# Attention's second product of batch 0 in plain float32 for all six head pairs

## The chip, the cores and the metric

The kernel runs on one core of one Trainium2 chip. The metric is the device time of one execution in microseconds (us), the median over the runs that were made of it. A profile is one execution taken by the hardware profiler; its own time stands beside its span, from the first to the last instruction. The names of the engines are those of the profile: PE is TensorE's matmul side, PEld its weight loads, DVE is VectorE, ACT is ScalarE, POOL is GpSimd, and SP is the queue that issues every DMA of this kernel.

## The reference

Attention over 4 batches, 12 heads, 448 positions and 64 channels, with RMS-normalised queries and keys; its output, 1792 rows of 768, then goes through two blocks of matrix products. Cut to what matters here:

```python
scores = scale * np.matmul(q_n, k_n.transpose(0, 1, 3, 2))
scores = scores - np.max(scores, axis=-1, keepdims=True)
attn = np.exp(scores)
attn = attn / (np.sum(attn, axis=-1, keepdims=True) + 1e-09)
attn_out = np.matmul(attn, v)            # "the second product"
x = attn_out.transpose(0, 2, 1, 3).reshape(B * S, H * D)
x = ((x @ w1) * (x @ w2)) @ w3 @ w_out   # layers 1 and 2
h = x @ w_in
out = (h * np.clip(h + 3.0, 0.0, 6.0) / 6.0) @ w_out2
```

## The kernel before, in words

The 48 heads are taken as 24 pairs (`NP`), six pairs (`HP`) to a batch, so pairs 0 to 5 are batch 0. The attention loop goes by steps: pair i has its eight score tiles (two heads, four chunks of 112 queries) in steps 8i to 8i+7, its seven transposes (`trans`) from step 8i+8 and its seven second products (`pv`) from step 8i+10. In each step the code writes down: the two score matmuls (L561, L562), DVE's scaling and row maximum (L568, L575), ACT's exponential (L580) of the step before, four 112 by 112 transposes on PE (L587) into a PSUM bank of the tag "t" (two banks), their way out of PSUM, and one second product.

Precision is kept by splitting. A float32 operand is written as a high part in float32r, rounded by ACT, and a low part in float32r, the rest, and matmuls are taken on the parts. For the second product of a pair that is not in `FULL` this means: ACT copies the transposed attention into `xh` (L596, function `thi`), DVE subtracts that from PSUM into `xl` (L606, `tlo`), `vsplit` makes V's high part on ACT (L549) and its low part on POOL (L550) from the tile `vr` into the tile `vo`, and `pv` multiplies 128 columns of V (high and low side by side) with `xh` (L639) and with `xl` (L640). Of seven products of a pair the fourth (`kb == 3`) holds the last 64 keys of both heads, 64 rows each (L627). Afterwards ACT copies one half of the result (L647, `xcopy`) and DVE adds the other half to it (L655, `xadd`).

For a pair in `FULL` the same functions take a shorter way: V is loaded straight into `vo` in float32 (`load_v`), `vsplit`, `tlo` and `xadd` do nothing, `xh` is float32, and `pv` is one float32 matmul with 64 columns of V (L635; for the fourth product L621). The tile tag `vo` has two buffers, `vr` has one.

Between the steps the code writes "filler": the products of the two linear layers that follow. First come the products of w3 and w_out (`wprime`, 128 by 384 columns, L81 to L83 on `woh`), then layers 1 and 2 of a batch (`layer1`, `layer2`, 448 columns, L81 to L83 on `xhl`), at a rate of so many us of matmul for each step. Layer 1 of batch 0 begins only when `wprime` is through and pairs 0 to 5 are ready (`xout` L664, `xsplit` L308). The weights for the filler arrive as 8-byte numbers and are converted on ACT (L137, L138), DVE (L140, L143), ACT (L203 or L287) and POOL (L205 or L289).

The order of the instructions on each engine is not the written one alone: a scheduler sets it by simulated times, buffers and the links that `issue_after` adds. After about 640 us the attention is over and the third and fourth layers take the rest.

Of the kernel before, what the change touches and what calls it, by code (L numbers as in the profile page):

```python
# [24 lines left out]
HP = H // 2  # L25
# [11 lines left out]
NH = DM // 2  # L37
XB = 7
TAGS = ("s", "t", "v", "f")
FULL = (0, 1)  # L40
LG = 8
AHEAD = 3
K3 = 12
# [4 lines left out]
def fused_kernel(ctx: ExitStack, tc: tile.TileContext, nat, qT, kT, vin, gq, gk,  # L48
# [358 lines left out]
    def attention(ap, rate):  # L407
        def full(i):
            return i in FULL

# [556 lines left out]
```

## Time and profile before

| what | value |
|---|---|
| median of 3 runs | 1238.3 us (1236.92 to 1243.6) |
| profiled execution: its own time | 1239.83 us |
| profiled execution: its span | 1238.1 us, mean granted clock 0.98 |
| PE busy | 1168.1 us, 94% of the span |
| DVE busy | 751.1 us, 61% |
| ACT busy | 727.8 us, 59% |
| POOL busy | 463.9 us, 37% |

Busy times are averages over stages with different limits. Matmuls are pipelined: one that is recorded as 0.37 us long can be followed by the next after 0.21 us, so the distance from start to start says what one costs, and not its recorded length.

### The profile page before, as it was taken

The numbers are of one execution on the slowest core, as the hardware profiler recorded it, in microseconds if no ns is written. First come the engines' busy times: TensorE is split into PE (matmuls) and PEld (weight loads), VectorE is DVE, ScalarE is ACT, GpSimd is POOL, SyncE is SP. The second block draws the span as 40 slices with busy tenths as digits, with TensorE's granted clock in tenths as the row PEclk, the third lists the DMA queues.
The fourth block names the chain that finished last, engine by engine and source line by source line (L and its number), as shares of the span: only waits on it lengthen the run. The fifth ranks groups of instructions, "written<-read, shape, count | busy, mean of one in ns | idle before, by whom it ended". The sixth has DMA issues, their size and how long they took to land.

```text
span 1238.1 us, 16937 instructions
## 1 busy us (share of the span) xinstructions
PE 1168.1 (94%) x5868; PEld 1024.0 (83%) x5868; DVE 751.1 (61%) x1474; ACT 727.8 (59%) x1401; POOL 463.9 (37%) x316
## 2 busy tenths in 40 slices
PE   3698998988899999999999999989999999999998
PEld 2457877777789999889998998779999999999997
DVE  6977988998767787667624436774433333343332
ACT  6887788888857677666534435664533443343332
POOL 3534234553522213221020005445545445455442
PEclk9798998998999999999999999999999999999999
DMA  7667666797987777764469963440200020001001
GB/s 277 204 215 237 193 184 205 247 291 260 307 299 239 224 238 224 244 224 174 145 253 410 342 236 127 154 153 1 89 1 1 1 90 1 1 1 45 1 1 45
DMA packets 64694, 203.73 MB, mean 165 GB/s; under 512 B 8544, under 2 KB 25440, under 8 KB 64608
## 3 DMA queue, kind: packets, MB, share of 16 engines
q1 hardware_dynamic: 64608, 202.65, 48.4%
q8 instruction: 46, 0.75, 0.2%
q14 instruction: 40, 0.33, 0.1%
HBM read 173.93 MB, written 28.68 MB: 164 GB/s over the span
## 4 chain that ended last, share of the span: by engine, by line
PE 62%; DMA 4%; DVE 4%; ACT 3%; issue 2%; POOL 0%; SPq 0%; ACTq 0%; POOLq 0%; DVEq 0%
PE bank L81 7%; PE bank L83 7%; PE bank L82 7%; PE acc L81 6%; PE acc L82 6%; PE acc L83 6%; PE h L81 5%; PE h L82 5%; PE h L83 5%; PE bank L587 2%; PE bank L561 1%; PE bank L562 1%; DVE wf L143 1%; PE bank L639 1%; PE bank L640 1%
## 5 line engine op out<-in xcount | busy, mean ns | idle before, releaser
L835 POOL TENSOR_TENSOR wis<-wf,wis 128x768 fp32r<-128x768 f32 x63 | 120.9, 1919 | 234.3 <-ACT wis L834 234.3
L907 DVE SCALAR_TENSOR_TENSOR u<-u,h 128x448 f32<-128x448 f32 x64 | 39.6, 619 | 212.3 <-ACT u L906 212.3
L835 POOL TENSOR_TENSOR wos<-wf,wos 128x768 fp32r<-128x768 f32 x64 | 119.0, 1860 | 98.1 <-ACT wos L834 98.1
L580 ACT ACTIVATE PP<-PP,mx 112x448 f32<-112x448 f32 x192 | 127.4, 665 | 38.9 <-DVE mx L575 34.3
L568 DVE CUSTOM_DVE_ANT_0 PP<-bank,rb,rq 112x448 f32<-112x448 f32 x192 | 129.3, 677 | 32.0 <-PE bank L562 25.2
L81 PE MATMUL bank<-xhl,ws 128*128 128x448 f32 x384 | 143.1, 373 | 3.7 <-ACT ws L287 2.2
L83 PE MATMUL bank<-xhl,ws 128*128 128x448 f32 x384 | 141.5, 369 | 3.7 <-POOL ws L289 3.7
L82 PE MATMUL acc<-g,wos 128*128 128x448 f32 x384 | 142.6, 371 | 2.3 <-DVE g L911 2.3
L83 PE MATMUL acc<-g,wos 128*128 128x448 f32 x384 | 141.9, 369 | 0.0
L82 PE MATMUL bank<-xhl,ws 128*128 128x448 f32 x384 | 141.2, 368 | 0.0
L81 PE MATMUL acc<-g,wos 128*128 128x448 f32 x384 | 138.8, 374 | 2.5 <-ACT g L910 2.5
L81 PE MATMUL h<-x2h,wis 128*128 128x448 f32 x378 | 139.2, 368 | 0.6 <-DVE u L907 0.6
L83 PE MATMUL h<-x2h,wis 128*128 128x448 f32 x378 | 137.7, 364 | 2.2 <-POOL wis L835 2.2
L82 PE MATMUL h<-x2h,wis 128*128 128x448 f32 x378 | 139.0, 368 | 0.0
L906 ACT ACTIVATE u<-h,half 128x448 f32<-128x448 f32 x64 | 40.6, 634 | 141.1 <-PE h L83 141.1
L911 DVE TENSOR_TENSOR g<-u,g 128x448 fp32r<-128x448 f32 x64 | 99.5, 1554 | 35.4 <-ACT g L910 35.4
L606 DVE TENSOR_TENSOR xl<-bank,xh 128x448 fp32r<-128x448 f32 x142 | 87.4, 617 | 30.0 <-ACT xh L596 28.3
L834 ACT ACTIVATE wos<-wf 128x768 fp32r<-128x768 f32 x64 | 54.0, 844 | 84.2 <-PE acc L83 84.0
L587 PEld LDWEIGHTS bank<-ident,PP 112*128 112x128 f32 x672 | 79.3, 143 | 28.0 <-issue 9.7
L596 ACT ACTIVATE xh<-bank 128x448 fp32r<-128x448 f32 (+1 forms) x156 | 83.1, 539 | 32.4 <-PE bank L587 30.8
L587 PE MATMUL bank<-ident,PP 112*128 112x112 f32 x672 | 96.0, 266 | 6.5 <-DVE xl L606 5.2
L561 PE MATMUL bank<-K,Q 128*112 128x448 f32 x192 | 77.1, 403 | 24.1 <-DVE mx L568 12.7
(128 smaller groups left out, 2755.7 us busy)
## 6 DMA issues: line engine op xcount, KB each, us to landing
ws<-w12d SPq DMA_DIRECT2D x48, 768.0 KB
ws<-wpd SPq DMA_DIRECT2D x32, 768.0 KB
raw<-in_w_dram SPq DMA_DIRECT2D x32, 384.0 KB
w12d<-ws SPq DMA_DIRECT2D x16, 768.0 KB
wr<-in_win_dram SPq DMA_DIRECT2D x16, 768.0 KB
wr<-in_wo_dram SPq DMA_DIRECT2D x16, 768.0 KB
qr<-in_qT_dram SPq DMA_DIRECT2D x24, 448.0 KB
kr<-in_kT_dram SPq DMA_DIRECT2D x24, 448.0 KB
```

Of the source, the lines that this page charges most:

```text
L81: nc.tensor.matmul(ps, lh, rh, start=first, stop=False)
L82: nc.tensor.matmul(ps, lh, rl, start=False, stop=False)
L83: return nc.tensor.matmul(ps, ll, rh, start=False, stop=last)
L561: nc.tensor.matmul(ps[:CP, :S], qs, k1[:, j, :], start=True, stop=False)
L568: anchors[8 * i + s].append(nc.vector.tensor_tensor_reduce(out=T["PP", i][:, c, sl], in0=ps[:CP, :S], in1=T["rb", i][:, sl], op0=ALU.mult, ...
L580: anchors[8 * i + s].append(nc.scalar.activation(v, v, AF.Exp, bias=T["m", i][:, 8 + s : 9 + s], accum_out=T["sum", i][:, s : s + 1]))
L587: nc.tensor.transpose(ps[:, c * CP : c * CP + CP], src[:, c, kb * P : kb * P + P], ident[:CP, :CP])
L596: nc.scalar.activation(hi, ps, AF.Copy)
L606: nc.vector.tensor_sub(lo, ps, hi)
L834: nc.scalar.activation(t[:, 0, :], wf[q], AF.Copy)
L835: nc.gpsimd.tensor_sub(t[:, 1, :], wf[q], t[:, 0, :])
L911: nc.vector.tensor_sub(g[:, 1, :], u, g[:, 0, :])
```

## The change

`FULL` names the pairs that take the float32 way. It held pairs 0 and 1; now it holds all six pairs of batch 0. Pairs 6 to 23 stay as they were, and no other line is touched.

```diff
-FULL = (0, 1)
+FULL = range(HP)
```

## Rows read from the trace of the kernel before

**Rows 1.** Stretches: length, then PE, PEld, DVE, ACT, POOL busy, clock, DMA.

```profile
110.00:140.00 30.00, 30.00 (x178) 27.76 (x177) 19.86 (x48) 19.37 (x42) 11.34 (x10) 1.00 0.77 233
140.00:182.00 42.00, 39.94 (x228) 34.10 (x227) 38.18 (x99) 33.45 (x74) 13.60 (x11) 1.00 0.58 180
182.00:200.00 18.00, 15.56 (x68) 11.85 (x67) 16.66 (x39) 13.42 (x33) 8.43 (x7) 0.72 0.53 174
200.00:350.00 150.00, 134.25 (x690) 110.11 (x689) 129.56 (x319) 127.08 (x286) 74.50 (x63) 0.98 0.82 273
350.00:640.00 290.00, 288.61 (x1599) 261.13 (x1598) 201.45 (x524) 188.26 (x406) 65.50 (x56) 1.00 0.66 218
```

**Rows 2.** Timeline of PE, a float32 product of pair 0: start, length, what.

```profile
74.31 0.33 PE L82 MATMUL bank<-woh,w 128*128 128x384 f32 x1
74.49 0.34 PE L83 MATMUL bank<-woh,w 128*128 128x384 f32 x1
74.76 0.97 PE L635 MATMUL bank<-xh,vo 128*64 128x448 f32 x2
75.65 0.60 PE L587 MATMUL bank<-ident,PP 112*128 112x112 f32 x4
```

**Rows 3.** Timeline of PE, split products of pair 3.

```profile
136.71 0.45 PE L640 MATMUL bank<-xl,vo 128*128 128x448 f32 x1
137.00 0.37 PE L639 MATMUL bank<-xh,vo 128*128 128x448 f32 x1
137.21 0.36 PE L561 MATMUL bank<-K,Q 128*112 128x448 f32 x1
```

**Rows 4.** Timeline of PE, the fourth product: pair 1 in float32, pair 4 split.

```profile
85.93 0.97 PE L621 MATMUL bank<-xh,vo 64*64 64x448 f32 x4
86.83 0.60 PE L587 MATMUL bank<-ident,PP 112*128 112x112 f32 x4
...
163.12 0.47 PE L627 MATMUL bank<-xh,vo 64*128 64x448 f32 x2
163.51 0.60 PE L587 MATMUL bank<-ident,PP 112*128 112x112 f32 x4
```

**Rows 5.** Groups by line, 100 to 200 us: busy, mean ns | idle before.

```profile
L606 DVE TENSOR_TENSOR xl<-bank,xh 128x448 fp32r<-128x448 f32 x29 | 17.9, 616 | 2.4 <-ACT xh L596 2.1
...
L550 POOL TENSOR_TENSOR vo<-vr,vo 128x512 fp32r<-128x512 f32 x4 | 5.5, 1379 | 31.4 <-DMA rsb<-rsd 14.1 <-ACT vo L549 10.1 <-issue 7.3
```

**Rows 6.** Waits of PE, 100 to 200 us: total, times, longest.

```profile
PE bank L587 <- DVE xl L606: 2.6, 3, 1.7
PE bank L640 <- DVE xl L606: 1.4, 2, 0.7
PE bank L83 <- POOL w L205: 1.1, 1, 1.1
PE bank L561 <- DVE mx L568: 0.8, 2, 0.4
```

**Rows 7.** Stretches at the low clock, and what lies before them.

```profile
102.00:107.60 5.60, 5.52 (x19) 5.33 (x20) 5.57 (x14) 5.60 (x11) 1.45 (x1) 0.50 0.54 177
186.40:196.40 10.00, 9.21 (x31) 6.77 (x32) 8.73 (x20) 7.29 (x19) 5.21 (x5) 0.50 0.68 236
97.20:102.10 4.90, 1.86 (x8) 0.68 (x6) 4.90 (x14) 4.85 (x13) 1.84 (x2) 0.88 0.79 270
183.60:186.40 2.80, 1.25 (x6) 0.65 (x4) 2.80 (x5) 2.80 (x7) 1.93 (x2) 0.97 0.65 169
```

**Rows 8.** Timeline of DVE and POOL: one DVE operation twice, and POOL beside it.

```profile
100.16 1.24 DVE L487 TENSOR_SCALAR rq<-rr 112x16 f32<-112x16 f32 x1
...
148.79 0.16 DVE L487 TENSOR_SCALAR rq<-rr 112x16 f32<-112x16 f32 x1
...
99.79 1.59 POOL L550 TENSOR_TENSOR vo<-vr,vo 128x512 fp32r<-128x512 f32 x1 [2.34 <-ACT vo L549]
```

**Rows 9.** Waits of the SP queue, 100 to 200 us.

```profile
SPq L89 <- DVE Q L534: 7.7, 1, 7.7
```

## Prediction

> **What bounds the kernel now.** I read the stretches first, because the mean over the span hides the stages [rows 1]. The products that change, of pairs 2 to 5, stand between 102 and 195 us. There PE is busy for 30.00 of 30 us from 110 to 140 and for 39.94 of 42 us up to 182, so PE sets the pace. From 182 to 200 us PE has only 15.56 of 18 us, at a mean clock of 0.72. DVE is nearly as full: 38.18 of 42 and 16.66 of 18 us. From 200 to 350 us no engine is full (PE 134.25, DVE 129.56, ACT 127.08 of 150), and from 350 to 640 us PE has 288.61 of 290. Next I read what PE waits for in this stage [rows 6]: 5.9 us in all, 4.0 of them for DVE's `xl`, which is what the change takes away. Then the clock [rows 7]: two stretches, 5.6 and 10.0 us long, run at 0.50, that is the lower level of 1.2 GHz. Before the first PE worked 1.86 of 4.90 us, before the second 1.25 of 2.80. So the stage is bound by PE, with gaps that DVE causes and that are followed by a slow clock. The change gives PE more work and DVE less, and the question is which counts for more.
>
> I take a delay or a gain at 200 us to reach the end in full: layer 1 of batch 0 can't begin before the filler of this stage is through, and from 350 us on PE has no room to catch up [rows 1].
>
> **PE's new work.** In `FULL` a product is one float32 matmul, recorded as two. From its start to the next instruction it takes 75.65 - 74.76 = 0.89 us, and it begins 0.27 us after a filler matmul, where filler follows filler after 0.18 us: 0.09 us at its entry [rows 2]. A split product is two matmuls, one after transposes with 0.29 us to the next and one with 0.21 us: 0.50 us, or 0.42 us where both follow other matmuls [rows 3]. So a product costs 0.89 - 0.50 = 0.39 us more at the least, 0.89 + 0.09 - 0.42 = 0.56 us at the most. I take 0.50, nearer the upper end, because both kinds of entry (after transposes and after filler) occur in this stage and the shown float32 product has filler ahead of it. The fourth product of a pair has four short matmuls in 0.90 us, where the split way has two passes of 0.39 us: 0.12 us more [rows 4]. A pair has six of the first kind and one of the second: 6 x 0.50 + 0.12 = 3.1 us, four pairs 12.5 us. The bounds are 4 x (6 x 0.39 + 0) = 9.4 and 4 x (6 x 0.56 + 0.12) = 13.9 us.
>
> The Trainium skill, in "FP8 and Floating Point Precision", section "TensorE Precision Notes", says that true float32 makes four passes through the array. Four passes of 0.21 us would be 0.84 us, and the four pairs would then cost 4 x (6 x 0.42 + 0.12) = 10.6 us by my estimate. The trace has two records and 0.89 us, somewhat more than that, and I go by the trace.
>
> **What DVE, ACT and POOL lose.** The four pairs drop 28 subtractions for `xl` (29 stand in the window, 0.616 us each, so 17.2 us) [rows 5]. They drop eight half additions in `xadd`, at most as long as these, so up to 4.9 us: 22 us of DVE in all. They drop the four splits of V, on POOL 4 x 1.38 = 5.5 us [rows 5], and on ACT four copies of the same tile. None of these engines is the bound, so I don't subtract their time. What counts is which of PE's gaps they made.
>
> First, the waits for `xl`: 4.0 us [rows 6]. The two before L640 (1.4 us) go, since that matmul goes. The three before L587 (2.6 us) are transposes that need a PSUM bank which DVE still reads. In the new way ACT is the last reader, and it is done earlier by about one subtraction, 0.62 us each. But a transpose can still wait for ACT's `xh`. I take 3.0 us as gain, between 1.4 and 4.0.
>
> The longest of them, 1.7 us at 102.08 us, has a second cause: an `rq` operation on DVE takes 1.24 us where the same one elsewhere takes 0.16, and POOL's split of V runs beside it [rows 8]. With the split gone, that 1.08 us goes as well. It is part of the same wait, so I don't add it.
>
> The Trainium skill, in "SBUF — State Buffer", section "SBUF: two separate sides", says that some DVE operations and a POOL operation exclude each other on a shared port for a whole instruction. These two rows agree with that.
>
> Second, the waits for a weight's low part from POOL and for a row maximum from DVE, 1.1 + 0.8 us [rows 6]. Both come late in DVE's order, and DVE would now be ahead. I take 1.5 us, between 0 and 1.9.
>
> Third, the clock. At 0.50 a stretch costs about half of PE's busy time in it: 5.52 / 2 = 2.8 us and 9.21 / 2 = 4.6 us, together 7.4 us less the waits inside, say 7 [rows 7]. If the gaps before them shrink, part of this goes. The first gap (97.2 to 102.1 us) is made mostly by work that stays: the normalisation of the next pair and the scores. The second (183.6 to 186.4) is made by a late weight and by `xl`. I take 1.3 us from the first and 2.0 from the second, 3.3 us, between 0 and 7.
>
> **The sum.** 12.5 - 3.0 - 1.5 - 3.3 = 4.7 us slower. On the profiled execution's own time of 1239.83 us that gives 1244.5. The median, 1238.3, is 1.5 us below that execution, so I predict 1243 us.
>
> **Moved waits.** V of pairs 2 to 5 is now loaded straight into `vo`, which has two buffers, and no longer into `vr`. So the load of pair i waits on the SP queue until pair i-2 has done its last product, and not until the split of pair i-1. Behind it in the queue stand the filler's weights, `qr` and `kr`, and the small transfers of the row sums. By the written order the buffer comes free in step 8i and the first use is in step 8i+10, so V itself isn't late. What the queue loses I set at nothing in the sum, because in this stage SP already waits once for 7.7 us [rows 9] and PE's list of waits names no transfer [rows 6]. If the cover goes, it is the weights that are late, and with them POOL's `w` and then filler on PE; that is the third rival below.
>
> The scheduler places instructions by simulated times, and it will place them anew. I can't see from the trace what that does. The gaps it could open or close are of the size of those in rows 6, so I leave 3 us to either side.
>
> **The rivals.** (1) PE pays in full, slower: the gaps for `xl` only turn into gaps for `xh`, and the clock falls as before. This needs ACT to be as late as DVE was; ACT is busy for 33.45 of 42 us, but 13.42 of 18 [rows 1]. Then 12.5 less 1.4 for the two L640, so about 11 us: 1249 us. For it speaks that PE has no room between 110 and 182 us.
>
> (2) DVE's relief wins, faster: DVE was what held the stage from 182 to 200 us, and with 22 us less work it no longer does. Then all of the waits go (5.9 us) and both slow stretches (7 us), and the float32 products cost their lower bound of 9.4: -3.5 us. If the 200 to 350 stretch, where DVE has 129.56 of 150 us, also begins with DVE ahead and recovers another 4 of PE's 15.75 idle us, it is -7.5 us: 1231. It decides from the point where the gaps recovered exceed 9.4 to 13.9 us. The Trainium skill, in "TensorE: Matmul & The Clock Gate", section "HAM oscillation — how this bites in real kernels", says that gaps in PE's work bring the slow clock, and that denser work keeps it fast. By that rule alone this rival's clock term would be right. The rows of the two stretches agree with the first half of it.
>
> (3) The queue: two of the four loads of V hold SP for about the 4 us that is half of its longest wait [rows 9], the weights come late, and PE waits 8 us more than in my sum: 1251 us. Against it: V is written down only two steps before the buffer comes free.
>
> **Chances and range.** My forecast, between 1236.5 and 1247, has 0.47; rival (1) 0.25, (2) 0.16, (3) 0.12. A change within 0.5% (6.2 us, 1232.1 to 1244.5) is about what a measurement of this kernel can't tell from none. From the forecast's share some 0.40 falls inside this and 0.07 above; rival (2) gives 0.15 below and 0.01 inside; a little of (1) also falls inside, 0.04. So faster 0.15, same 0.45, slower 0.40. The range of 8 in 10 goes from rival (2), 1231, to a little beyond (3), 1254.
>
> **What would show it.** Right: L635 with 72 records instead of 24 and 0.89 us from each to the next; L606 with 114 instead of 142 and L549 with 18 instead of 22; PE's waits for `xl` between 100 and 200 us gone; the first score of pair 9, which now stands near 228 us, later by about 5 us, and the same shift at the end. Wrong: a shift there of more than 9 us (rival 1 or 3, told apart by waits on weights) or a negative one (rival 2, with the clock at 1.00 from 182 to 200 us); or a shift at 230 us that is gone at 350, which would mean that my step "reaches the end in full" fails.

## The result, and the profile after

The changed kernel takes 1247.01 us, median of 10 runs (1241.6 to 1251.19), beside 1239.34 us for the kernel before, run on the same chips (10 runs, 1234.26 to 1244.3). The ratio is 1.0059, with a 95% interval of 1.0036 to 1.0083: 7.3 us slower (0.0059 x 1239.3), between 4.5 and 10.3. The profiled execution has a span of 1247.5 us and 1249.72 us of its own time; it is 9.4 us above the span of the one before.

First the stretches, with the columns of [rows 1].

```profile
110.00:140.00 30.00, 30.00 (x151) 21.70 (x151) 18.41 (x42) 19.04 (x42) 8.99 (x7) 1.00 0.70 219
140.00:182.00 42.00, 42.00 (x206) 28.50 (x206) 26.21 (x71) 32.71 (x71) 12.29 (x11) 1.00 0.57 175
182.00:200.00 18.00, 18.00 (x96) 13.75 (x96) 15.97 (x41) 15.48 (x37) 11.56 (x9) 1.00 0.60 197
200.00:350.00 150.00, 131.67 (x660) 108.74 (x659) 130.60 (x296) 121.69 (x270) 68.72 (x58) 0.94 0.79 263
350.00:640.00 290.00, 286.95 (x1591) 257.82 (x1590) 206.18 (x542) 192.19 (x416) 67.69 (x57) 1.00 0.67 219
```

Where the products changed, PE is now full to the last digit, at the full clock: from 182 to 200 us 18.00 of 18 us at 1.00, where it had 15.56 at 0.72. The list of PE's waits from 100 to 200 us, which had 5.9 us [rows 6], has no line left. DVE fell from 38.18 to 26.21 us in the second stretch. Then it turns: from 200 to 350 us PE works less than before (131.67 against 134.25 us), at a lower clock (0.94 against 0.98).

The counts and the price are as foretold. The records of the three lines, shortest, median and longest in ns, then a float32 product in the timeline of PE:

```profile
L635 PE MATMUL bank<-xh,vo x72: 539/590/1009, 32.4 to 192.1; 128*64 128x448 f32 x72
...
L606 DVE TENSOR_TENSOR xl<-bank,xh x114: 571/618/626, 196.6 to 635.5; 128x448 fp32r<-128x448 f32 x114
...
L549 ACT ACTIVATE vo<-vr x18: 613/620/662, 169.3 to 597.6; 128x512 fp32r<-128x512 f32 x18
```

```profile
130.12 0.97 PE L635 MATMUL bank<-xh,vo 128*64 128x448 f32 x2
131.01 0.44 PE L83 MATMUL bank<-woh,w 128*128 128x384 f32 x1
```

131.01 - 130.12 = 0.89 us, as in [rows 2].

To see where the 9.4 us arise I cut both traces at 80 us and at three events that both have: PE's first matmul of layer 1, the first score of pair 14, and PE's first matmul on `wos` (`acc<-g,wos`), which I call the third layer. The columns are those of [rows 1]; first before, then after.

```profile
80.00:214.20 134.20, 124.11 (x651) 101.53 (x649) 114.19 (x288) 110.23 (x244) 52.70 (x42) 0.94 0.64 203
214.20:378.60 164.40, 149.55 (x773) 124.97 (x772) 135.87 (x329) 130.38 (x293) 74.42 (x63) 0.98 0.82 274
378.60:755.10 376.50, 373.25 (x1995) 339.05 (x1995) 228.16 (x534) 216.77 (x434) 69.30 (x57) 1.00 0.70 244
```

```profile
80.00:221.50 141.50, 133.89 (x675) 96.00 (x674) 106.55 (x271) 114.44 (x251) 51.35 (x40) 0.99 0.65 203
221.50:385.70 164.20, 148.74 (x751) 124.77 (x750) 135.79 (x312) 128.04 (x283) 71.30 (x61) 0.95 0.79 264
385.70:764.70 379.00, 373.60 (x1993) 338.42 (x1992) 227.68 (x532) 215.51 (x435) 69.31 (x57) 1.00 0.70 243
```

The idle time of PE is length less busy. At 0.50 of the clock half of the busy time is lost, so (1 - clock) x busy is what the clock costs, good to some 0.7 us since the clock has two digits. I call the two together the loss, and the rest of the length work.

| stage | idle + clock, before | idle + clock, after | loss | work |
|---|---|---|---|---|
| 1: 80 us to layer 1 | 10.1 + 7.4 | 7.6 + 1.3 | -8.6 | +15.9 |
| 2: to pair 14 | 14.8 + 3.0 | 15.5 + 7.4 | +5.1 | -5.3 |
| 3: to the third layer | 3.2 + 0 | 5.4 + 0 | +2.2 | +0.3 |

Together: work +10.9, loss -1.3, so 9.6 us later at the third layer (764.7 against 755.1). That work moves from stage 2 to stage 1 is a matter of the cut: layer 1 waits for the filler before it, and attention has gone further by then. The groups of PE in stage 1, before and after (records, then busy us and mean ns), show it:

```profile
L587 PE MATMUL bank<-ident,PP 112*128 112x112 f32 x156 | 23.8, 280 | 3.6 <-DVE xl L606 2.6 <-ACT xh L596 0.9
L561 PE MATMUL bank<-K,Q 128*112 128x448 f32 x47 | 19.2, 409 | 2.8 <-DVE mx L568 2.8
```

```profile
L587 PE MATMUL bank<-ident,PP 112*128 112x112 f32 x168 | 24.3, 265 | 2.7 <-ACT xh L596 1.5 <-DVE xl L606 1.3
L561 PE MATMUL bank<-K,Q 128*112 128x448 f32 x50 | 20.0, 401 | 4.1 <-DVE mx L568 4.1
```

12 more transposes and 3 more scores lie before layer 1, which itself begins 7.3 us later (221.5 against 214.2). So stage 1 recovers what I had forecast, and stages 2 and 3 lose 7.3 us that were not lost before. In stage 2 that is hardly idle time, 15.5 against 14.8 us, but the slow clock, 7.4 against 3.0. Over whole executions the clock gives nothing back: the mean granted clock of the changed kernel is 0.981 over its ten runs, and that of the kernel before 0.980 to 0.981 wherever it ran beside the runs below. PE's waits in stage 2 for weights (L81, L83) and for DVE's row maximum (L561), before and after:

```profile
PE bank L83 <- POOL ws L289: 3.7, 3, 2.5
...
PE bank L81 <- ACT ws L287: 2.2, 3, 0.9
PE bank L561 <- DVE mx L568: 1.3, 3, 1.0
```

```profile
PE bank L561 <- DVE mx L568: 6.2, 6, 3.1
...
PE bank L81 <- ACT ws L287: 1.8, 1, 1.8
...
PE bank L83 <- POOL ws L289: 0.2, 1, 0.2
```

The first new hole there, in windows of the changed kernel and in its timeline of PE:

```profile
235.90:239.20 3.30, 0.23 (x2) 0.00 (x0) 3.24 (x8) 1.98 (x5) 3.30 (x4) 0.74 0.89 262
238.00:244.20 6.20, 4.99 (x13) 4.40 (x14) 6.13 (x20) 2.60 (x5) 2.79 (x3) 0.50 0.95 342
```

```profile
239.21 0.71 PE L561 MATMUL bank<-K,Q 128*112 128x448 f32 x1 [3.09 <-DVE mx L568]
```

PE stands for 3.09 us for a score bank that DVE reads, DVE being busy for 3.24 of 3.30 us, and 6.2 us at 0.50 follow. Just behind it the SP queue stands, in the timeline of SP and in its list of waits:

```profile
241.94 0.42 SPq L89 DMA_DIRECT2D w12d<-ws  x1
251.46 0.32 SPq L89 DMA_DIRECT2D rkd<-rks  x1
...
254.40 0.54 SPq L89 DMA_DIRECT2D raw<-in_w_dram  x1
```

```profile
SPq L89 <- DVE rss L512: 9.2, 1, 9.2
```

A 7 KB transfer of key factors waits 9.2 us for DVE, with weights behind it. PE's waits for weights are nevertheless shorter in this stage than before, 2.0 us against 5.9.

### The profile page after: what moved, and what is told of

Read it like the earlier page. It is cut to its first block, busy times and chain, and to the rows that moved or that the text cites. A ratio compares the mean times of both kernels' runs of the same rounds, so it can differ in the third digit from the quotient of the medians.

```text
span 1247.5 us, 16863 instructions
## 1 busy us (share of the span) xinstructions
PE 1176.0 (94%) x5868; PEld 1016.7 (81%) x5868; DVE 743.4 (60%) x1438; ACT 727.3 (58%) x1397; POOL 459.3 (37%) x312
## 4 chain that ended last, share of the span: by engine, by line
PE 66%; DMA 12%; DVE 7%; ACT 7%; issue 5%; POOL 2%; SPq 1%; ACTq 0%; POOLq 0%; DVEq 0%
PE bank L81 8%; PE bank L83 8%; PE bank L82 8%; PE acc L82 5%; PE acc L83 5%; PE acc L81 5%; PE h L81 5%; PE h L82 5%; PE h L83 5%; PE bank L587 3%; DMA wr<-in_win_dram 2%; DMA raw<-in_w_dram 2%; DMA wr<-in_wo_dram 2%; PE bank L561 2%; PE bank L562 2%
## 5 line engine op out<-in xcount | busy, mean ns | idle before, releaser
L81 PE MATMUL bank<-xhl,ws 128*128 128x448 f32 x384 | 144.2, 376 | 3.7 <-ACT bs L316 1.9
L83 PE MATMUL bank<-xhl,ws 128*128 128x448 f32 x384 | 142.9, 372 | 0.3 <-POOL ws L289 0.2
L83 PE MATMUL acc<-g,wos 128*128 128x448 f32 x384 | 141.7, 369 | 0.0
L81 PE MATMUL acc<-g,wos 128*128 128x448 f32 x384 | 137.5, 370 | 4.0 <-ACT g L910 4.0
L81 PE MATMUL h<-x2h,wis 128*128 128x448 f32 x378 | 139.0, 368 | 1.2 <-DVE u L907 1.2
L83 PE MATMUL h<-x2h,wis 128*128 128x448 f32 x378 | 137.7, 364 | 2.3 <-POOL wis L835 2.3
L561 PE MATMUL bank<-K,Q 128*112 128x448 f32 x192 | 77.2, 403 | 30.0 <-DVE mx L568 18.8
L664 POOL TENSOR_TENSOR xs<-xs,rsb 128x448 f32<-128x448 f32 x24 | 28.0, 1166 | 195.0 <-DMA rsb<-rsd 148.9
```

What stands on the lines that cost most here:

```text
L81: nc.tensor.matmul(ps, lh, rh, start=first, stop=False)
L83: return nc.tensor.matmul(ps, ll, rh, start=False, stop=last)
L561: nc.tensor.matmul(ps[:CP, :S], qs, k1[:, j, :], start=True, stop=False)
```

## The experiments

Two theories at the start. **Theory A**: the loss is PE's added work in stage 1 less the relief there, and it is carried to the end. **Theory B**: what stage 1 hands over is small; how the scheduler's new order of stage 2 happens to fall decides the time. All kernels are timed against the kernel before on the same chip, so the ratios compare and the medians of different rows do so less well. The table gives their medians, and the loss in stages 1 and 2 from their one profiled execution each, cut and reckoned as above, with the work from 80 us up to pair 14 (length less loss).

| run | float32 pairs beyond 0, 1 | us | ratio to before, 95% | loss 1 | loss 2 | work |
|---|---|---|---|---|---|---|
| before | none | | 1 | 17.5 | 17.8 | 263.3 |
| changed | 2, 3, 4, 5 | 1247.01 | 1.0059 [1.0036, 1.0083] | 8.9 | 22.9 | 273.9 |
| e1 | 2 to 5, no relief | 1242.85 | 1.0014 [1.0000, 1.0029] | 10.6 | 17.0 | 273.0 |
| e2 | none, relief only | 1233.04 | 0.9940 [0.9920, 0.9959] | 11.7 | 26.1 | 257.7 |
| e3 | 2, 3 | 1245.69 | 1.0033 [1.0015, 1.0051] | 14.0 | 21.4 | 267.1 |
| e4 | 4, 5 | 1232.37 | 0.9932 [0.9912, 0.9952] | 7.0 | 20.7 | 266.2 |
| e5 | 2 to 5, other queue | 1254.03 | 1.0102 [1.0073, 1.0130] | 7.8 | 25.7 | 281.1 |
| e6 | none, other queue | 1242.88 | 1.0011 [0.9996, 1.0026] | 17.2 | 22.2 | 264.2 |
| e7 | 2 to 5, pace 1.10 | 1249.02 | 1.0053 [1.0033, 1.0073] | 12.1 | 28.8 | 276.5 |
| e8 | none, pace 1.10 | 1244.20 | 1.0013 [0.9995, 1.0030] | 18.4 | 24.4 | 265.2 |
| e9 | 2, 5 | 1242.41 | 1.0011 [0.9993, 1.0029] | 10.9 | 25.1 | 267.0 |
| e10 | 3, 4 | 1240.89 | 0.9996 [0.9979, 1.0014] | 9.7 | 16.6 | 271.2 |
| e11 | 5 | 1248.07 | 1.0050 [1.0027, 1.0072] | 8.9 | 31.2 | 264.1 |
| e12 | 4, 5, pace 1.10 | 1240.36 | 0.9985 [0.9968, 1.0002] | 6.9 | 27.6 | 272.2 |

Not all of the work column compares. In e7, e8 and e12 the cut at pair 14 holds 18 more filler matmuls than in the others. And 80 us is a fixed time: the fifth score of pair 2, which has the same matmuls behind it in every kernel, stands at 78.74 us before and between 78.3 and 80.9 us elsewhere, in e5 at 83.91. And one execution is not the median: the profiled one of e11 took 1243.5 us and that of e9 1248.58, some 5 us below and 6 us above their medians. A loss of one kernel alone carries little; what repeats down the column carries more: the three kernels without added float32 pairs and without relief (before, e6, e8) lose 17.2 to 18.4 us in stage 1, all others 6.9 to 14.0.

**e1: PE's work without the relief.** Pairs 2 to 5 keep the split of V and the subtraction `xl`, though no product uses `xl` or V's low part. Since no second matmul reads `xl`, PE's wait for it there is gone (1.4 us before [rows 6]), and `xadd` is away, as the expectation says; so this is the change without most of the relief.

```diff
+LATE = (2, 3, 4, 5)
 def load_v: if full(i):
+    if i in LATE: load into "vr" as before
 vsplit:
+    if full(i) and i in LATE: copy on ACT and subtract on POOL as before
-lo = None if full(i) else ap.tile(... "xl" ...)
+lo = None if full(i) and i not in LATE else ap.tile(... "xl" ...)
```

> Pairs 2 to 5 take the float32 products, but VectorE still writes xl for them, ScalarE and GpSimd still split V (nobody reads the low parts), and V is loaded by the old way through vr; only the eight xadd stay away. Theory A (float32 products cost PE 12 to 13 us, and only the relief of VectorE gives some of it back): slower than the kernel before by 10 to 16 us, so 2 to 8 us slower than the changed kernel, with waits of PE for xl back between 100 and 200 us. Theory B (the loss comes from the newly planned order after 215 us, PE's extra work is hidden anyway): within 4 us of the changed kernel on either side.

**e2: the relief without PE's work.** Split products stay, but the second matmul of pairs 2 to 5 takes the high part `xh` again. The low part of attention is left out for these pairs.

```diff
-lo = None if full(i) else ap.tile(... "xl" ...)
+lo = None if full(i) or i in LATE else ap.tile(... "xl" ...)
 pv:
+lo = hi if i in LATE else lo
```

> Pairs 2 to 5 keep the split products and the split of V, but the second matmul takes xh again and VectorE writes no xl for them (the low part of the attention is left out of the result). Theory A: PE loses its 4.0 us of waits for xl and part of the 7 us at the low clock and pays nothing: 5 to 9 us faster than the kernel before. Theory B: the gain up to 215 us is there, but the stretch from 215 to 350 us comes out anywhere: between 8 us faster and 5 us slower.

Stage 1 in the windows of e1, then of e2:

```profile
80.00:220.60 140.60, 132.69 (x656) 93.85 (x656) 112.23 (x284) 110.28 (x243) 54.35 (x42) 0.98 0.63 198
```

```profile
80.00:204.40 124.40, 117.41 (x655) 100.93 (x654) 97.56 (x262) 108.95 (x243) 53.51 (x44) 0.96 0.71 221
```

I read the share of the relief here. In e1 DVE has 112.23 us of work in stage 1, nearly the 114.19 of before, and PE's waits for `xl` are back as theory A had it (2.0 us between 100 and 200 us); its loss falls to 10.6 us all the same. In e2, with DVE at 97.56 us, it falls to 11.7; with both to 8.9. So the gaps close in either way: with DVE quicker, or with more work on PE. That what PE waits for has then come while it works is the likely reason, which no run isolates. The two do not add. e1 ends 0.45% faster than the changed kernel by the ratios, some 5.6 us, where theory A had it slower; theory B, within 4 us, is missed by less. e2 is 7.4 us faster than before, within theory A's 5 to 9, with 9.8 us gained in stage 1.

The work of e2 is 5.6 us below that of before, though it issues as many matmuls. Part of it is in the products themselves: with both matmuls on `xh` the second follows the first directly, and a product of 128 rows takes 0.45 us where it took 0.53 (means between 102 and 200 us, over matmuls with no gap and no slow clock). For 24 products that is 1.9 us; the rest stays open.

**e3 and e4: two of the four pairs.** `FULL = (0, 1, 2, 3)` and `FULL = (0, 1, 4, 5)`.

> FULL holds pairs 0 to 3, half of the change. Theory A: half of the changed kernel's loss, 3 to 5 us slower than before. Theory B: no order by the number of pairs; anything from 6 us faster to 9 us slower, with the filler of the first stage late by no more than 2 us at its end.

> FULL holds pairs 0, 1, 4 and 5: half of the change, at the other two pairs. Theory A: 2 to 5 us slower than before, a little less than with pairs 2 and 3, because the gaps of PE that are there to be filled lie late in the stage (182 to 200 us). Theory B: as for pairs 0 to 3, anything from 6 us faster to 9 us slower, and not the same as with pairs 2 and 3.

The same added work gives +0.33% and -0.68%, and four pairs give +0.59%: not a function of the count. e3 lies where theory A had it, 4.1 us over before. e4 is faster than both kernels, by 8.4 us than the one before (0.0068 x 1241.5), which neither theory allowed for.

**e5 and e6: is it the blocked queue?** The transfers `rkd<-rks` and `rsd<-rss` go out from GpSimd's queue, in the changed kernel and in the one before.

```diff
-dma(rkd[...], sb[: 8 * n, :])
+nc.gpsimd.dma_start(rkd[...], sb[: 8 * n, :])
...
-dma(rsd[i]..., sb)
+nc.gpsimd.dma_start(rsd[i]..., sb)
```

> The changed kernel, with the two small transfers of the row sums and of the key factors issued from GpSimd's queue, no longer from SyncE's, where one of them stood for 9.2 us with raw weight loads behind it. Theory A (the loss is PE's added work in the first stage, less the relief there, and is carried to the end): nothing changes at the start of layer 1, so 1247 us as the changed kernel, within 2. Theory B (the first stage's shift is made good or made worse in the second stage by the order there, and this blocked queue is the place): the raw loads stand some 9 us earlier, the slow clock after 238 us goes, and the time is 1240 to 1243 us. If the time falls but the kernel before gains as much from the same edit, the queue is a general cost and not this change's.

> The kernel before, with the same two small transfers issued from GpSimd's queue. It is the control to the run on the changed kernel. Theory A: as the kernel before, 1239 to 1241 us. Theory B: as the kernel before within 2 us, because its SyncE queue had no raw weight loads behind the blocked transfer; a gain of over 4 us would say that the queue costs the kernel before as much.

The kernel before doesn't move, and the changed kernel gets slower still, 1.02% over before, outside both theories. The trace says where: e5 is 5.6 us behind the changed kernel at the fifth score of pair 2 (83.91 against 78.34 us), before any changed pair, 5.7 us at layer 1 and 5.6 us at the end of the profiled executions (1253.1 against 1247.5). From that score on both take 1169.2 us. So in these two executions the whole difference arises in the first 84 us, and behind that moving the two transfers neither costs nor gives back anything: this one wait is not what costs the time. The queue as such is not cleared by it, since in e5 it stands elsewhere, in its waits from 215 to 300 us:

```profile
SPq L89 <- ACT K L540: 9.2, 3, 5.6
SPq L89 <- POOL vo L550: 8.3, 1, 8.3
```

**e7 and e8: another pace of the filler before layer 1.** One number sets the pace of the filler (us of matmul for each step) until `wprime` is through, in the changed kernel and in the one before.

```diff
 def rate(t):
     if "pool" not in L:      # until layer 1 is opened
-        return 1.05, 2
+        return 1.10, 2
```

The expectations below, and that of e12, take this number for the pace after stage 1. It is the pace of stage 1: in e8's trace 285 matmuls of `wprime` stand before the first score of pair 6, where the kernel before has 279, and 375 before the sixth of pair 7, where it has 363. So stage 1 is written in another order too, and not only what follows.

> The changed kernel, with the pace of the filler in the stages after the first set to 1.10 instead of 1.05. The work is the same and the first stage is written in the same order; only the order from about 215 us on is planned anew. Theory A: 1247 us within 2, and the same 7 to 9 us over the kernel before at this pace. Theory B: the plan of the second stage decides, so the time moves by 3 us or more, up or down, and the distance to the kernel before at the same pace is another one.

> The kernel before, with the same pace of 1.10. Theory A: 1240 us within 2, so that the changed kernel at this pace is 6 to 9 us above it. Theory B: also moves by some us, by another amount than the changed kernel.

Both stay where they were: 1.0053 against 1.0059, 1.0013 against 1. This one went for theory A rather than B: the time of the changed kernel moves by less than 3 us, and its distance to its base keeps its sign and most of its size under another plan of both stages, 0.4%, some 5 us, if less than the 6 to 9 that I expected.

**e9 to e11: the place of the pair.** With e4 in hand I formed **theory C**: PE's work is always paid, and what comes back is bounded by the holes that PE has at the pair's place (pairs 2 and 5 stand at the two slow stretches of [rows 7], pairs 3 and 4 where PE is full). **Theory P**: each pair has a price of its own. `FULL = (0, 1, 2, 5)`, `(0, 1, 3, 4)` and `(0, 1, 5)`.

> Float32 products for pairs 0, 1, 2 and 5. Before, PE's two holes with the slow clock behind them stand at the start of pair 2 (97 to 108 us) and at the end of pair 5 (184 to 196 us), and between 110 and 182 us, pairs 3 and 4, PE is full. Theory C (the added PE work of some 3 us for a pair is always paid, and what comes back is bounded by the idle time and slow clock that PE has at the place of the pair): two pairs with a hole, 6 us paid and 6 to 9 us back, 1236 to 1241 us, so the kernel before or a little faster, and faster than pairs 3 and 4. Theory P (every pair has its own price whatever the others are, from the runs with pairs 2, 3 and 4, 5: about +2 and -4.5 us each): 1238 to 1240 us. Theory B (the new plan scatters the time): anywhere from 1233 to 1249 us, with no relation to the pairs' place.

> Float32 products for pairs 0, 1, 3 and 4, which stand where PE is full and waits for little. Theory C: 6 us paid and 0 to 3 back, 1244 to 1248 us, though the work is that of the runs with pairs 4 and 5 and with pairs 2 and 5. In the trace the slow clock behind 184 us stays. Theory P: 1238 to 1240 us. Theory B: anywhere from 1233 to 1249 us.

> Float32 products for pairs 0, 1 and 5 alone. Theory C: 3 us paid; the hole and the slow clock at 184 to 196 us, some 6 us, come back, so 1236 to 1240 us, as good as pairs 4 and 5 or better. Theory P: about 4.5 us faster than before, 1236 to 1238 us. Theory A (the loss goes by the count of pairs): 1242 to 1244 us.

Theory C's order is missed: the pairs at the holes give +0.11%, the pairs away from them -0.04%, and pair 5 alone, which was to do as well as 4 and 5, +0.50%. The slow clock behind 184 us, which was to stay in e10, is gone there (1.00 in each 4 us from 176 to 204 us). P fails too, since 4 and 5 together give -0.68% and 5 alone +0.50%, and so does theory A for e11, some 6 us over before where it had 3. In stage 1 the loss falls to between 8.9 and 10.9 us in all three, wherever the pairs stand.

**e12: the best version at another pace.** e4 with the pace of e7.

> The kernel with float32 products for pairs 0, 1, 4 and 5 (0.7% faster than the kernel before), with the filler's pace after the first stage at 1.10 instead of 1.05: the same work, and the stages from about 215 us on planned anew. Theory P (a pair has a price by its place, pairs 4 and 5 a good one): it stays 0.5 to 0.9% faster than before, 1231 to 1236 us. Theory B (how the second stage's plan meets the state that the first leaves decides, and that kernel met it well): the time goes back to those of the other kernels with two pairs, 1238 to 1246 us, with 22 us or more of idle time and slow clock of PE between the start of layer 1 and 390 us, where that kernel had 20.

It goes back to 0.9985, as theory B had it. Stage 1, and the stretch that differs most in stage 2, in the windows of e4 and then of e12:

```profile
80.00:211.50 131.50, 125.77 (x664) 98.04 (x663) 106.94 (x277) 110.65 (x244) 52.10 (x41) 0.99 0.66 211
...
320.00:350.00 30.00, 30.00 (x164) 26.20 (x165) 21.45 (x51) 22.19 (x52) 10.92 (x11) 1.00 0.91 310
```

```profile
80.00:209.10 129.10, 123.38 (x652) 95.96 (x651) 107.24 (x268) 108.78 (x241) 50.75 (x41) 0.99 0.70 214
...
320.00:350.00 30.00, 24.48 (x113) 20.15 (x112) 22.65 (x56) 21.17 (x49) 16.14 (x14) 0.89 0.91 304
```

Stage 1 is alike in its loss, 7.0 and 6.9 us, and e12, whose filler is written at the higher pace there, reaches layer 1 2.4 us sooner; from 320 to 350 us PE is full in e4 and idle for 5.5 us in e12, and over stage 2 the loss is 20.7 against 27.6 us. The same work, once planned otherwise, costs 0.53% more, some 6.6 us. The gain of e4 is real for that kernel, but most of it belongs to its plan and not to its pairs.

## Why the prediction was right, and which step failed

The forecast was 1243 us, 4.7 above the profiled execution; measured are 7.3 above before, with 4.5 to 10.3 as interval. The time lies in the range. The kernel is slower by 0.59%, a little more than the 0.5% that I counted as the same, though the interval (0.36 to 0.83%) reaches below that. That the forecast came as near as 3 us is luck in part: the terms of my sum, as measured, give 2.3 us, and the rest comes from a term that I had put at nothing with 3 us to either side. Step by step:

- **PE's new work**, 12.5 us: the trace has 10.9, of which 10.6 up to pair 14. Over the seven kernels at the old pace and queues (changed, e1, e3, e4, e9, e10, e11) the work up to pair 14 rises by 2.3 us for each added pair, or 2.2 if it is taken from the fifth score of pair 2 on, where I had 3.1 and a lower bound of 2.35. A float32 product costs the 0.89 us that I took. The split product was priced too low: in the kernel before, its matmuls of 128 rows between 102 and 200 us took 0.26 us each from start to start (16 and 19 of them, with no gap and no slow clock), so 0.53 and not 0.50 us, and 0.42 was hardly met. The fourth product costs nothing more, 0.90 us against 0.93. With the entry of 0.09 that gives 6 x 0.45 = 2.7 us a pair; the rest of the distance to 2.3 stays open. By the Trainium skill's four passes ("FP8 and Floating Point Precision", section "TensorE Precision Notes") my estimate had been 10.6 us, which is nearer, but by chance, since it takes 0.42 us for the split product.
- **Gains in stage 1**, 3.0 + 1.5 + 3.3 = 7.8 us: the loss fell by 8.6 us, of which the clock gave 6.1 and idle time 2.5. The size was right, the split was not: the clock gave 6.1 where I had 3.3, and idle time 2.5 where I had 4.5. The cause was only half right: I put it all down to DVE's relief, and e1 shows 6.9 us of it (17.5 to 10.6) without any `xl` or split of V taken away, though 1.4 us of this go with the matmul that read `xl`.
- **"A delay or a gain at 200 us reaches the end in full"** is the step that failed. On the face of it it holds: the delay is 7.3 us at layer 1, 7.1 at pair 14, 9.6 at the third layer. But of the 7.3 us (15.9 - 8.6) at layer 1, 5.3 are work that attention has done ahead and that stage 2 then has less to do. Stage 2 gives next to none of it back, because it loses 5.1 us more than before, 4.4 of them by the slow clock, and stage 3 loses another 2.2. By my sum alone, with the measured work, 10.9 - 8.6 = 2.3 us should have reached the end. In e2 stage 1 gains 9.8 us (204.4 against 214.2), and 7.4 us are left in the median.
- **The scheduler's new order**, "3 us to either side", is the term that was mis-sized, and it is what fills the difference. e4 and e12 differ by 0.53% with the same work; five kernels with two added pairs lie between -0.68 and +0.33%, 12.5 us apart, and no count, place or pair orders them. It is as large as what the change itself does. On the mean four pairs are slower than two: +0.57% (changed, e1, e5, e7) against -0.09% (e3, e4, e9, e10, e12). That is 8 us for two more pairs, where their work is under 5, and one pair (e11, +0.50%) does not fit in at all. So these means give no price of a pair.
- **The queue** (rival 3) did not come. The loads of V hold SP for 1.0 us between 100 and 200 us. The queue waits longer for POOL's conversion of weights, 16.2 us in all where it was 5.5 before, but PE waits for nothing in that time. The waits of SP there, beside [rows 9]:

```profile
SPq L89 <- POOL w L205: 16.2, 6, 5.8
...
SPq L89 <- PE bank L635: 1.0, 2, 0.6
```

- **Rival 1** (PE pays in full) fails in stage 1, where the waits and most of the slow clock went; its 11 us lie above the interval. **Rival 2** was right there: the clock is 1.00 from 182 to 200 us, which I had named as its sign, and the waits are all gone. Its second half, that the stretch from 200 to 350 us would begin with DVE ahead and recover more, went the other way, and so its time did. The rule that it leaned on in the Trainium skill ("TensorE: Matmul & The Clock Gate", section "HAM oscillation — how this bites in real kernels") agrees with the trace in both places: denser work kept the clock from 182 to 200 us at 1.00, where it had been 0.72, and the hole at 236 us was followed by 0.50. Its chances were off in one point: by its own first sum, -3.5 us, rival 2 ends at 1234.8 us, inside what I called the same, and yet I gave 0.15 of its 0.16 to faster.
- **What would show it**: the counts, 0.89 us and the waits came as told. The first score of pair 9 was a bad marker. It stands at 227.38 us, where it stood at 227.59, because attention runs ahead while the filler falls behind; the delay shows at the first matmul of layer 1, and again at pair 14, 7.1 us later.

What stays open is which decision of the order in stage 2 costs the time. The one transfer that blocked the queue is ruled out as the main cause by e5 and by PE's shorter waits for weights; the holes for DVE's row maximum come to 6.2 us in stage 2, against 1.3 before, but no run took them away alone.

## What to carry to other kernels

Where one engine sets the pace and still has gaps, added work on it and relief of the engine it waits for can close the same gaps: here the loss of 17.5 us fell to 10.6 with the work, to 11.7 with the relief, and to 8.9 with both. Cost them together. A change of a few microseconds in a kernel whose order is planned by a scheduler must be tried under two or three plans of the same work (another pace, another choice of tiles) before its sign is believed; here another plan of the same work was worth 6.6 us (e4 and e12) and the change 7.3, and under the one other plan that was tried the change kept its sign, at some 5 us. Read in the code, and then in the trace, which stretch a number governs before an experiment leans on it: the pace of e7, e8 and e12 was not that of the stage it was meant for. To see where a shift arises, cut both traces at the same events and set work, idle time and cost of the clock side by side for each stage, and choose events of every stream of work, since one may run ahead while the other falls behind.

## What the runs showed that I had not expected

A kernel with 10.9 us more matmul work had a lower loss of clock in the stage that holds it: 1.3 us against 7.4. And moving two transfers of 7 and 3.5 KB to another queue left one kernel as it was (1.0011) and made its near twin slower, from 1.0059 to 1.0102 over before. In the profiled executions all of that slowing stands in the first 84 us, before the first of the changed products.
